# Middle weight bits by 16-bit copies on ScalarE, the first chunk's tap sums by float32 products on TensorE, and a rewritten opening list

## The chip, the cores and the metric

The kernel runs on one core of a Trainium2 chip. The metric is the device time of one execution in microseconds (us). The engines of the core are named as in the profile: PE is TensorE (products; PEld its weight loads), DVE is VectorE, ACT is ScalarE, POOL is GpSimd, and SP is SyncE, which issues most DMAs.

## The reference

The input x holds 8 sequences of 4160 rows of 192 numbers. Each row is replaced by a weighted sum over itself and the six rows before it, with seven weights ("taps") for each of 8 heads of 24 columns, after a softmax over the taps. Then three matrix products of 192 to 768 columns are taken, their elementwise maximum, and a product back to 192 columns. The matrices come in as 64-bit floats.

```
w = exp(weight_gen - max(weight_gen));  w = w / (sum(w) + 1e-9)     # over the 7 taps
out = einsum('bshk,bskhg->bshg', w, x_unf)                           # x_unf: rows s-6 .. s
h = maximum(maximum(out @ w1, out @ w2), out @ w3)
return h @ w_out
```

## The kernel before

**Tiling.** The 33,280 rows are 260 tiles of 128, one row on each partition; four tiles are a chunk of 512 rows, and there are 65 chunks. The rows of a partition are neighbours in the sequence, so that a tap is a shift along the tile xt. Inputs are loaded for a "super" at a time: the first is chunk 0 alone, the others are three chunks each.

**A chunk's path.** `softmax` works on a super (VectorE for the maxima, sums and reciprocals, GpSimd for the subtraction and the scaling, ScalarE for the exponentials). `product` (x in the list) multiplies a tile by its taps on GpSimd into r, 192 columns by 7 taps with the taps innermost, of which there are three buffers. `total` (+) sums the taps on VectorE into acc. `transpose` (t) turns acc so that the columns lie on the partitions: for chunks 0 to 2 on TensorE against a unit matrix, later on VectorE and ScalarE. `parts` (p) divides the result into float32 parts of fewer bits, xa_hi, xa_lo, xb and xc. `up` multiplies the parts by the weights' parts, nine steps of 18 products of 512 columns for a chunk: each product stands on 64 of 128 partitions, and the second half of the rows follows the first, so that two streams of products run beside each other. `maximum` takes the maxima (m) and their parts h_hi and h_lo; `down` multiplies by w_out and stores.

**The weights** come as 64-bit floats, viewed as two 32-bit words, low and high. `split` makes of each the part hi with 12 bits and the part lo with the next 24. It is called 18 times, all in the opening: nine times for wa (a in the list; 256 columns, from the tiles h_hi and raw_a, which hold raw words until later), three times for wb (b; 384 columns, from h_lo), six times for wo (d; 192 columns, from room). In each, ScalarE takes the absolute value (L467); three VectorE instructions make hi (L469, L471, L476), which ScalarE casts into place (L481); three more gather the 24 bits from both words (L483, L488) and the exponent (L492); ScalarE scales (L494) and GpSimd multiplies (L495). For wb four more casts on ScalarE put hi on both halves of the partitions (L550).

**Order.** Work is written in ticks, 22 to a chunk. What the steady table of ticks doesn't set, for chunks 0 to 4, stands in `OPENING`, a list by hand of the steps at each tick; -1 is before the first product. A name in it advances its step by one stage. `pin` keeps the order so written on each engine, and every engine works through its own queue in order. In `up`, the terms of one result are products in a fixed order.

Of the kernel before, what the change touches and what calls it, by code (L numbers as in the profile page):

```python
# [13 lines left out]
F32 = mybir.dt.float32  # L14
F32R = mybir.dt.float32r
U32 = mybir.dt.uint32
AF = mybir.ActivationFunctionType
ALU = mybir.AluOpType
AX = mybir.AxisListType

P = 128
# [3 lines left out]

OPENING = {
    -1: (
        "x0.0 s0 x0.1 a0 s0 a0 a0 x0.2 a0 a2 t0 +0.0 a2 b0 +0.1 a1 b0 b0 a1 +0.3 s1 a3 b0 a1 "
        "a2 s1 a1 +0.2 t0 b1 s1 x0.3"
    ),  # L30
    0: "a6 a4 a2 a3 a6",
    1: "a6 a3 b0 t0 t0",
    2: "b1 a6 s0",
    3: "a4 a5 a3",
    4: "b1 a5",
    6: "b2 +1.0 a5 x1.1 x1.0",
    7: "x1.2 s1 a4",
    8: "+1.1",
    9: "a5 b2 x1.3",
    10: "b2 b2 b1 p0",  # L40
    11: "s0 t1 +1.2",
    12: "a4 +1.3",
    14: "b1 p0",
    16: "a7 a7 a8 p1",
    17: "a7 t1",
    18: "s2 d1 d1 a8 p1",
    19: "p1 b2 a8 d2 t1",
    20: "d2 p0 d1",
    21: "d0",
    22: "d0",  # L50
    24: "a7 +2.0 d0",
    25: "d2 +2.1 d1",
    26: "d3 t1",
    27: "d0 x2.1 d3 d5 d2",
    28: "d3 x2.2",
    29: "x2.3 d3 a8 d4",
    30: "d4 x2.0",
    31: "d5",
    32: "+2.2 d4 d5",
    33: "t2 +2.3 t2 t2",  # L60
    34: "s2",
    35: "x3.0 x3.2 p2",
    36: "d4",
    38: "d5 p2 p2",
    42: "x3.1",
    43: "t3 t3",
    46: "+3.3 +3.2 +3.1 +3.0 t2",
    48: "t3",
    49: "s2",
    52: "x4.1",  # L70
    54: "t3",
    56: "x4.0 p3",
    57: "x3.3",
    58: "p3 t3 s2",
    59: "t3",
    61: "+4.1",
    66: "x4.2",
    67: "x4.3",
    68: "t3",
    69: "p3",  # L80
    74: "+4.3 +4.2",
    77: "+4.0",
}


# [7 lines left out]
LOAD = (5, 5)  # L93

ON_TENSOR = 3


@with_exitstack
def lightconv_maxout_kernel(
# [25 lines left out]
    nc = tc.nc  # L125
    B, S, D = x.shape
    H, K = weight_gen.shape[2:]
# [36 lines left out]
    ident = const.tile([P, P], F32, name="ident")  # L164
    wa_hi = const.tile([P, NJ, 3, P], F32R, name="wa_hi")
    wa_lo = const.tile([P, NJ, 3, P], F32R, name="wa_lo")
    wb_hi = const.tile([P, NJ, 3, P], F32R, name="wb_hi")
# [8 lines left out]
    state = {}  # L176

    def pin(ins):

        tc.keep_in_program_order(ins)  # L180
        return ins
# [28 lines left out]
    def softmax(s):  # L210
# [10 lines left out]
        yield  # L221
        pin(nc.scalar.activation(w3v, w3v, AF.Exp))
        yield
# [10 lines left out]
    def product(c, t):  # L234

        s = super_of[c]
        a, n = chunks[c]
        la = a - chunks[supers[s][0]][0]
        xt, wt = state["x", s], state["w", s]
        if t == 0:  # L240
            state["acc", c] = att.tile([P, TC, D], F32, name="acc")

        r = att.tile([P, D, K], F32, name="r", bufs=3)
        state["r", c, t] = r
        pin(
            nc.gpsimd.tensor_tensor(  # L246
                r.rearrange("p (h g) k -> p k h g", g=G),
                xt[:, la + t : la + t + K].rearrange("p k (h g) -> p k h g", g=G),
                wt[:, la + t]
                .rearrange("p (h k) -> p k h", k=K)  # L250
                .unsqueeze(3)
                .broadcast_to([P, K, H, G]),
                op=ALU.mult,
            )
        )

    def total(c, t):

        r = state.pop(("r", c, t))
        pin(  # L260
            nc.vector.tensor_reduce(  # L261
                state["acc", c][:, t], r, axis=AX.X, op=ALU.add
            )
        )

    def transpose(c):


        acc = state["acc", c]
        if c < ON_TENSOR:  # L270
            pa, pb = (ps.tile([P, CH], F32, name="ph") for _ in range(2))
            pb = pb[:DB]
            state["p", c] = pa, pb
            for t in range(TC):
                to = slice(t * P, (t + 1) * P)
                pin(nc.tensor.transpose(pa[:, to], acc[:, t, :P], ident))
                pin(nc.tensor.transpose(pb[:, to], acc[:, t, P:], ident))
                yield
            return
        v = xtp.tile([P, NJ * D * 2], F32, name="room", bufs=1)  # L280
        pa, pb = v[:, :CH], v[DB:, CH : 2 * CH]
        state["p", c] = pa, pb
        blocks = v[:, 2 * CH : 2 * CH + TC * D].rearrange("p (t d) -> p t d", t=TC)
        pin(nc.vector.transpose(blocks, acc))  # L284
        yield
        for f in range(0, D, 32):
            to = pa[f : f + 32] if f < P else pb[f - P : f - P + 32]
            to = to.rearrange("f (t p) -> f t p", t=TC)
            for p in range(0, P, 32):
                pin(nc.scalar.copy(to[:, :, p : p + 32], blocks[p : p + 32, :, f : f + 32]))  # L290
            yield

    def parts(c):
# [8 lines left out]

        eng, at = (nc.vector, halves[0]) if c < ON_TENSOR else (nc.gpsimd, halves[1])
        pin(eng.tensor_tensor(xa_lo, pa, xa_hi.bitcast(F32), op=ALU.subtract))  # L304
# [38 lines left out]
    def up(step, half):  # L343
        c, jp, i = step
        N = chunks[c][1] * P
        xa_hi, xa_lo, xb, xc = state["xT", c]
        for odd in range(2):
            j = 2 * jp + odd
            terms = [(wa_hi[:, j, i], xa_hi), (wa_hi[:, j, i], xa_lo), (wa_lo[:, j, i], xa_hi)]
            terms.append((wb_hi[:, j, i], xb))  # L350
            if half == odd:
                terms.append((wb_lo[:, jp, i], xc))
            if half == 0:
                state["ph", step, odd] = ps.tile([P, CH], F32, name="ph")
            terms = [(N, w, v[:, :N]) for w, v in terms]
            yield from product_of(state["ph", step, odd], terms, half, (step, odd))
            if half == 1:
                maximum(step, odd)
# [89 lines left out]

    words = [w.bitcast(U32) for w in (w1, w2, w3, w_out)]

    def split(raw, hi, lo):

        low, high = raw[..., 0], raw[..., 1]


        n = int(np.prod(raw.shape[1:-1]))
        if 2 * n <= CH:
            both = ps.tile([P, CH], F32, name="ph")
            u, l = both[:, :n], both[:, n : 2 * n]
        else:  # L460
            u, l = (ps.tile([P, CH], F32, name="ph")[:, :n] for _ in range(2))
        e, f = (prep.tile([P, NU], F32, name=name, bufs=3)[:, :n] for name in ("e", "f"))
        if len(raw.shape) == 4:
            u, l, e, f = (v.rearrange("p (i n) -> p i n", n=P) for v in (u, l, e, f))
        ui, li, ei = (v.bitcast(U32) for v in (u, l, e))

        pin(nc.scalar.activation(u, high.bitcast(F32), AF.Abs))  # L467
        yield
        pin(nc.vector.tensor_scalar(u, u, F_MAX, F_MIN, op0=ALU.min, op1=ALU.max))  # L469
        pin(  # L470
            nc.vector.tensor_scalar(  # L471
                ui, ui, 3, 0x3FFFF000, op0=ALU.logical_shift_left, op1=ALU.bitwise_and
            )
        )
        pin(
            nc.vector.scalar_tensor_tensor(  # L476
                ui, high, 0xC0000000, ui, op0=ALU.bitwise_and, op1=ALU.bitwise_or
            )
        )
        yield  # L480
        pin(nc.scalar.copy(hi, u))  # L481
        pin(
            nc.vector.tensor_scalar(  # L483
                li, high, 0x1FF, 15, op0=ALU.bitwise_and, op1=ALU.logical_shift_left
            )
        )
        pin(
            nc.vector.scalar_tensor_tensor(  # L488
                li, low, 17, li, op0=ALU.logical_shift_right, op1=ALU.bitwise_or
            )  # L490
        )
        pin(nc.vector.tensor_scalar(ei, ui, 0xFF800000, None, op0=ALU.bitwise_and))  # L492
        yield
        pin(nc.scalar.activation(f, li, AF.Copy, scale=2.0**-35))  # L494
        pin(nc.gpsimd.tensor_tensor(lo, f, e, op=ALU.mult))  # L495


    room = [
        hp.tile([P, NJ, CH], F32R, name=name).bitcast(U32).rearrange("p j n -> p (j n)")
        for name in ("h_hi", "h_lo")  # L500
# [4 lines left out]
        for r in (  # L505
            room[0][:, :SA],
            room[0][:, SA : 2 * SA],
            prep.tile([P, SA], U32, name="raw_a", bufs=1),
        )
    ]  # L510
    raw_b = room[1][:, : NJ * SB // 2].rearrange("p (j i n w) -> p j i n w", j=NJ // 2, i=3, w=2)
    raw_down = xtp.tile([P, NJ * D * 2], F32, name="room", bufs=1).bitcast(U32)
    raw_down = raw_down.rearrange("p (j n w) -> p j n w", j=NJ, w=2)
# [119 lines left out]
    for c in range(NC + 1):  # L633
        for tick in range(TICKS):
# [10 lines left out]
            k, odd = divmod(tick - (TC if tick >= 2 * DOWN_AT else 0), 2)  # L645
# [5 lines left out]
            if c == NC:  # L651
# [4 lines left out]
                elif tick >= 2 * DOWN_AT + TC and tick < 2 * DOWN_AT + 2 * TC:  # L656
                    t = tick - 2 * DOWN_AT - TC
# [44 lines left out]
```

## Time and profile before

| | us |
|---|---|
| median of 3 runs (1714.65 to 1714.75) | 1714.68 |
| profiled execution | 1714.73 |
| its span | 1712.9 |
| PE busy | 1668.9 (97%) |
| POOL busy | 1427.9 (83%) |
| ACT busy | 1138.6 (66%) |
| DVE busy | 1135.5 (66%) |

Busy time is the time in which an instruction of the engine ran; register, branch and DMA-issuing instructions don't count. Shares are over the whole span, so they mix the opening, in which weights are made ready, with the main stage. [...]

### The profile page before, as it was taken

What the parts mean: (1) busy time and instruction counts of PE and PEld (TensorE: products, weight loads), DVE (VectorE), ACT (ScalarE), POOL (GpSimd) and SP (SyncE); (2) the same over time, 40 slices, a digit from 0 to 9 for tenths busy, and PEclk for the clock granted to TensorE, in tenths of its full rate; (3) what the DMA queues carried; (4) which work ended last, traced back from release to release, by engine and by line L of the source; (5) the groups of instructions that cost most, each with busy time, mean ns of one, the idle gap of its engine ahead of it and who ended that gap; (6) DMA issues with size and microseconds to landing.
All of it is one profiled execution on the core that took longest, in us unless ns stands there. A gap on an engine that the chain in (4) does not pass through costs nothing.

```text
span 1712.9 us, 42123 instructions
## 1 busy us (share of the span) xinstructions
PE 1668.9 (97%) x16794; PEld 1639.7 (96%) x16794; DVE 1135.5 (66%) x1570; ACT 1138.6 (66%) x2878; POOL 1427.9 (83%) x844
## 2 busy tenths in 40 slices
PE   3799999999999999999999999999999999999999
PEld 2589999999999999999999999999999999999999
DVE  7967666666666666766666666666666666666653
ACT  3556667667667667666766766766766766676672
POOL 5888888989888888888888898988889888888872
PEclk9999999999999999999999999999999999999999
DMA  7010101101010110101010110101011010101000
GB/s 234 1 69 11 69 20 60 69 20 60 20 70 10 70 43 38 69 20 67 13 70 20 60 69 20 60 20 69 11 69 49 31 69 20 69 11 46 20 11 29
DMA packets 20422, 79.50 MB, mean 46 GB/s; under 512 B 2321, under 2 KB 5129, under 8 KB 17537
## 3 DMA queue, kind: packets, MB, share of 16 engines
q1 hardware_dynamic: 20104, 76.54, 11.8%
q8 instruction: 131, 2.15, 0.5%
q14 instruction: 67, 0.54, 0.1%
q10 hardware_dynamic: 120, 0.28, 0.1%
HBM read 51.25 MB, written 25.56 MB: 45 GB/s over the span
## 4 chain that ended last, share of the span: by engine, by line
PE 94%; DVE 4%; DMA 1%; issue 0%; SPq 0%; ACT 0%; DVEq 0%; ACTq 0%
PE ph L329 94%; DVE acc L261 1%; DVE m L378 1%; DVE ph L471 0%; DVE e L492 0%; DVE ph L476 0%; DMA h_lo<-in_moe_w_dram 0%; DVE ph L488 0%; DVE ph L469 0%; DVE ph L483 0%; DMA xt<-in_x_dram 0%; SPq L526 0%; DVE red L215 0%; SPq L518 0%; DVE xb L309 0%
## 5 line engine op out<-in xcount | busy, mean ns | idle before, releaser
L246 POOL TENSOR_TENSOR r<-xt,wt 128x1344 f32<-128x1344 f32 x260 | 721.8, 2817 | 0.7 <-DMA xt<-in_x_dram 0.4
L378 DVE TENSOR_TENSOR m<-ph,m 128x512 f32<-128x512 f32 x780 | 522.8, 685 | 215.4 <-PE ph L329 115.8
L385 POOL TENSOR_TENSOR h_lo<-m,h_hi 128x512 fp32r<-128x512 f32 x390 | 503.3, 1302 | 169.3 <-ACT h_hi L381 164.5
L329 PE MATMUL ph<-xa_hi,wa_hi 64*128 64x512 f32 x2340 | 627.5, 390 | 5.6 <-ACT f L494 3.4
L329 PE MATMUL ph<-xa_lo,wa_hi 64*128 64x512 f32 x2340 | 624.8, 388 | 2.5 <-DVE xa_lo L304 2.5
L329 PE MATMUL ph<-xa_hi,wa_lo 64*128 64x512 f32 x2340 | 624.3, 388 | 2.8 <-POOL wa_lo L495 2.7
L329 PE MATMUL ph<-xb,wb_hi 64*128 64x512 f32 x2340 | 623.9, 387 | 0.0
L329 PE MATMUL ph<-wo,h_hi 64*128 64x384 f32 x3120 | 596.1, 358 | 0.0
L329 PE MATMUL ph<-wo,h_lo 64*128 64x192 f32 x3120 | 554.9, 249 | 0.0
L381 ACT CAST h_hi<-m 128x512 fp32r<-128x512 f32 x390 | 242.0, 621 | 403.9 <-DVE m L378 400.9
L329 PEld LDWEIGHTS ph<-wo,h_hi 64*128 64x128 f32 x3120 | 486.3, 184 | 7.3 <-POOL wo L495 0.2
L329 PEld LDWEIGHTS ph<-wo,h_lo 64*128 64x128 f32 x3120 | 484.8, 187 | 0.1
L261 DVE TENSOR_REDUCE acc<-r 128x192 f32<-128x1344 f32 x260 | 401.9, 1547 | 109.7 <-POOL r L246 109.7
L290 ACT COPY room<-room 32x128 f32<-32x128 f32 x1488 | 440.6, 296 | 26.7 <-DVE room L284 8.5
L329 PE MATMUL ph<-xc,wb_lo 64*128 64x512 f32 x1170 | 453.3, 387 | 1.4 <-POOL wb_lo L495 1.4
L329 PEld LDWEIGHTS ph<-xa_hi,wa_hi 64*128 64x128 f32 x2340 | 364.3, 185 | 12.7 <-ACT f L494 4.2
L329 PEld LDWEIGHTS ph<-xa_hi,wa_lo 64*128 64x128 f32 x2340 | 357.6, 185 | 6.8 <-POOL wa_lo L495 4.4
L329 PEld LDWEIGHTS ph<-xa_lo,wa_hi 64*128 64x128 f32 x2340 | 357.6, 185 | 5.1 <-DVE xa_lo L304 3.0
L329 PEld LDWEIGHTS ph<-xb,wb_hi 64*128 64x128 f32 x2340 | 357.8, 185 | 2.5
L376 ACT COPY m<-ph 128x512 f32<-128x512 f32 x390 | 222.0, 586 | 57.1 <-PE ph L329 49.6
L411 DVE TENSOR_TENSOR o<-ph,ob 128x192 f32<-128x192 f32 x260 | 86.5, 353 | 237.5 <-ACT ob L410 237.5
L329 PEld LDWEIGHTS ph<-xc,wb_lo 64*128 64x128 f32 x1170 | 216.0, 185 | 3.6 <-POOL wb_lo L495 1.8
(57 smaller groups left out, 699.7 us busy)
## 6 DMA issues: line engine op xcount, KB each, us to landing
xt<-in_x_dram SPq DMA_DIRECT2D x20, 1728.0 KB, 6.8
out_dram<-o SPq DMA_DIRECT2D x64, 384.0 KB, 2.3
wt<-in_weight_gen_dram SPq DMA_DIRECT2D x21, 336.0 KB, 3.0
h_hi<-in_moe_w_dram SPq DMA_DIRECT2D x6, 256.0 KB, 5.5
xt<-in_x_dram SPq DMA_DIRECT2D x1, 1536.0 KB, 9.3
h_lo<-in_moe_w_dram SPq DMA_DIRECT2D x6, 192.0 KB, 5.6
room<-in_moe_w_out_dram SPq DMA_DIRECT2D x1, 1152.0 KB, 7.6
xt<-in_x_dram SPq DMA_DIRECT2D x1, 960.0 KB, 5.1
```

Source lines behind the costliest of these rows:

```text
L246: nc.gpsimd.tensor_tensor(r.rearrange("p (h g) k -> p k h g", g=G), xt[:, la + t : la + t + K].rearrange("p k (h g) -> p k h g", g=G), wt[ ...
L261: nc.vector.tensor_reduce(state["acc", c][:, t], r, axis=AX.X, op=ALU.add)
L290: pin(nc.scalar.copy(to[:, :, p : p + 32], blocks[p : p + 32, :, f : f + 32]))
L329: ins = nc.tensor.matmul(ph[:, :n], w[h], v[h], start=begins and half == 0 and q == 0, stop=ends and half == 1 and q == len(terms) - 1,)
L376: pin(nc.scalar.copy(m[:, :N], ph[:, :N]))
L378: pin(nc.vector.tensor_tensor(m[:, :N], ph[:, :N], m[:, :N], op=ALU.max))
L381: later(1, lambda: pin(nc.scalar.copy(hi, m[:, :N])))
L385: nc.gpsimd.tensor_tensor(lo, m[:, :N], hi.bitcast(F32), op=ALU.subtract)
L411: pin(nc.vector.tensor_tensor(o[:, t], po[:, :D], ob, op=ALU.add))
```

## The change

There are four edits. `split` no longer shifts and joins the two words on VectorE. ScalarE copies the two middle 16-bit quarters of each 64-bit number, as numbers of 16 bits, into the tile f, and one VectorE instruction masks them there; the factor of the scaling is halved, since the bits now stand one place higher. For chunk 0 `total` does nothing: `transpose` takes the taps' products r themselves as the weights of seven float32 products with the unit matrix, which add up in PSUM, twice for each tile (128 and 64 columns). In `up` the product with wa_lo goes to the end of its terms. And `OPENING` is written anew from tick -1 to 82.

```diff
 OPENING = {
     -1: (
-        "x0.0 s0 x0.1 a0 s0 a0 a0 x0.2 a0 a2 t0 +0.0 a2 b0 +0.1 a1 b0 b0 a1 +0.3 s1 a3 b0 a1 "
-        "a2 s1 a1 +0.2 t0 b1 s1 x0.3"
+        "x0.0 x0.1 a0 a0 a2 x0.3 t0 a0 a1 a0 a2 t0 a2 x0.2 t0 b0 b0 a2 b0 s1 a1 a1 b0 t0 s1 "
+        "b1 a1 s1 a3 s0"
     ),
...
+SUMS_ON_TENSOR = (0,)
...
-        if t == 0:
+        if t == 0 and c not in SUMS_ON_TENSOR:
             state["acc", c] = att.tile([P, TC, D], F32, name="acc")
...
     def total(c, t):
 
+        if c in SUMS_ON_TENSOR:
+            return
...
-                pin(nc.tensor.transpose(pa[:, to], acc[:, t, :P], ident))
-                pin(nc.tensor.transpose(pb[:, to], acc[:, t, P:], ident))
+                if c in SUMS_ON_TENSOR:
+                    r = state.pop(("r", c, t))
+                    for k in range(K):
+                        for ph, f in ((pa, slice(0, P)), (pb, slice(P, D))):
+                            pin(
+                                nc.tensor.matmul(
+                                    ph[:, to], r[:, f, k], ident, start=k == 0, stop=k == K - 1
+                                )
+                            )
+                else:
+                    pin(nc.tensor.transpose(pa[:, to], acc[:, t, :P], ident))
+                    pin(nc.tensor.transpose(pb[:, to], acc[:, t, P:], ident))
...
-            terms = [(wa_hi[:, j, i], xa_hi), (wa_hi[:, j, i], xa_lo), (wa_lo[:, j, i], xa_hi)]
-            terms.append((wb_hi[:, j, i], xb))
+            terms = [(wa_hi[:, j, i], xa_hi), (wa_hi[:, j, i], xa_lo), (wb_hi[:, j, i], xb)]
             if half == odd:
                 terms.append((wb_lo[:, jp, i], xc))
+            terms.append((wa_lo[:, j, i], xa_hi))
...
         pin(nc.scalar.activation(u, high.bitcast(F32), AF.Abs))
         yield
+        flat = raw.rearrange("p i n w -> p (i n) w") if len(raw.shape) == 4 else raw
+        pin(
+            nc.scalar.copy(
+                f_words.bitcast(U16).rearrange("p (n h) -> p n h", h=2),
+                flat.bitcast(U16)[..., 1:3],
+            )
+        )
...
-        pin(
-            nc.vector.tensor_scalar(
-                li, high, 0x1FF, 15, op0=ALU.bitwise_and, op1=ALU.logical_shift_left
-            )
-        )
-        pin(
-            nc.vector.scalar_tensor_tensor(
-                li, low, 17, li, op0=ALU.logical_shift_right, op1=ALU.bitwise_or
-            )
-        )
+        pin(nc.vector.tensor_scalar(li, f.bitcast(U32), 0x01FFFFFE, None, op0=ALU.bitwise_and))
...
-        pin(nc.scalar.activation(f, li, AF.Copy, scale=2.0**-35))
+        pin(nc.scalar.activation(f, li, AF.Copy, scale=2.0**-36))
```

On VectorE, from the end of the first wa split to the first wb split (the wb words are in h_lo), there stood before:

```order
L492 TENSOR_SCALAR e<-ph 128x256
L261 TENSOR_REDUCE acc<-r 128x192
L469 TENSOR_SCALAR ph<-ph 128x256
L471 TENSOR_SCALAR ph<-ph 128x256
L476 SCALAR_TENSOR_TENSOR ph<-h_hi,ph 128x256
L261 TENSOR_REDUCE acc<-r 128x192
L469 TENSOR_SCALAR ph<-ph 128x384
L471 TENSOR_SCALAR ph<-ph 128x384
L476 SCALAR_TENSOR_TENSOR ph<-h_lo,ph 128x384
L483 TENSOR_SCALAR ph<-h_lo 128x384
L488 SCALAR_TENSOR_TENSOR ph<-h_lo,ph 128x384
L492 TENSOR_SCALAR e<-ph 128x384
```

Now there stands on VectorE, at the same place:

```order
L506 TENSOR_SCALAR e<-ph 128x256
L492 TENSOR_SCALAR ph<-ph 128x256
L494 TENSOR_SCALAR ph<-ph 128x256
L499 SCALAR_TENSOR_TENSOR ph<-h_hi,ph 128x256
L505 TENSOR_SCALAR ph<-f 128x256
L506 TENSOR_SCALAR e<-ph 128x256
L492 TENSOR_SCALAR ph<-ph 128x384
L494 TENSOR_SCALAR ph<-ph 128x384
L499 SCALAR_TENSOR_TENSOR ph<-h_lo,ph 128x384
L505 TENSOR_SCALAR ph<-f 128x384
L506 TENSOR_SCALAR e<-ph 128x384
L216 TENSOR_REDUCE red<-wt 128x96
```

The two sums of chunk 0 are gone, the second wa split is finished ahead of the wb split, both splits have five instructions and not six, and the maximum of the second softmax (red) follows at once.

On ScalarE, around the first wb split, from its absolute value on, there stood before, with the exponentials of the second softmax as the last row:

```order
L467 ACTIVATE ph<-h_lo 128x384
L467 ACTIVATE ph<-h_hi 128x256
L481 CAST hi<-ph 128x384
L467 ACTIVATE ph<-h_hi 128x256
L494 ACTIVATE f<-ph 128x384
L550 CAST wb_hi<-hi 64x384 x4
L481 CAST wa_hi<-ph 128x2x128 x2
L222 ACTIVATE wt<-wt 128x672
```

Now, on ScalarE at that place:

```order
L481 ACTIVATE ph<-h_lo 128x384
L487 COPY f<-h_lo 128x768
L508 ACTIVATE f<-ph 128x256
L504 CAST hi<-ph 128x384
L487 COPY f<-h_hi 128x512
L504 CAST wa_hi<-ph 128x2x128
L508 ACTIVATE f<-ph 128x384
L564 CAST wb_hi<-hi 64x384 x4
L223 ACTIVATE wt<-wt 128x672
```

Copies of 16-bit numbers have come in, and the cast of a wa split (wa_hi) stands ahead of the wb casts, no longer behind them.

On TensorE, where the transposes of chunk 0 end and its first products begin, there stood before (xa, xb and xc are the parts of chunk 0):

```order
L276 MATMUL ph<-ident,acc 128x128
L277 MATMUL ph<-ident,acc 64x128
L329 MATMUL ph<-xa_hi,wa_hi 128x512
L329 MATMUL ph<-xa_lo,wa_hi 128x512
L329 MATMUL ph<-xa_hi,wa_lo 128x512
L329 MATMUL ph<-xb,wb_hi 128x512
L329 MATMUL ph<-xc,wb_lo 128x512
```

Now, on TensorE there, the last two of 56 float32 products and then the first terms:

```order
L284 MATMUL ph<-ident,r 128x128
L284 MATMUL ph<-ident,r 64x128
L342 MATMUL ph<-xa_hi,wa_hi 128x512
L342 MATMUL ph<-xa_lo,wa_hi 128x512
L342 MATMUL ph<-xb,wb_hi 128x512
L342 MATMUL ph<-xc,wb_lo 128x512
L342 MATMUL ph<-xa_hi,wa_lo 128x512
```

The transposes of chunk 0 have become products that read r, and wa_lo is now read last.

## Rows read from the trace of the kernel before

**Rows 1.** Stretches: start:end and length, busy us (instructions) by engine, granted clock, DMA.

```profile
30.00:40.00 10.00, 7.46 (x28) 5.48 (x29) 9.38 (x22) 4.11 (x10) 3.71 (x4) 1.00 0.67 259
40.00:50.00 10.00, 6.17 (x44) 4.10 (x43) 9.79 (x18) 5.35 (x12) 9.12 (x6) 1.00 0.00 0
...
60.00:70.00 10.00, 6.68 (x40) 4.46 (x42) 9.52 (x23) 6.00 (x14) 7.45 (x6) 0.83 0.00 0
...
200.00:1600.00 1400.00, 1400.00 (x14242) 1394.03 (x14240) 926.53 (x1237) 961.59 (x2446) 1208.20 (x700) 1.00 0.11 44
```

**Rows 2.** Chain of work that ended last: start us, us, what.

```profile
10.65 6.09 DMA h_lo<-in_moe_w_dram
...
17.44 0.58 DVE ph L469
...
175.85 1533.65 PE ph L329 x12937
```

**Rows 3.** Waits of DVE from 9 to 92 us: us in total, times, longest.

```profile
DVE ph L469 <- ACT ph L467: 3.3, 2, 2.3
```

**Rows 4.** DVE in order of time: start us, us, engine, line, operation.

```profile
20.64 0.42 DVE L469 TENSOR_SCALAR ph<-ph 128x256 f32<-128x256 f32 x1
...
42.08 0.68 DVE L378 TENSOR_TENSOR m<-ph,m 128x512 f32<-128x512 f32 x1
...
58.92 0.43 DVE L488 SCALAR_TENSOR_TENSOR ph<-raw_a,ph 128x256 uint32<-128x256 uint32 x1
59.38 0.42 DVE L492 TENSOR_SCALAR e<-ph 128x256 uint32<-128x256 uint32 x1
...
87.53 1.54 DVE L261 TENSOR_REDUCE acc<-r 128x192 f32<-128x1344 f32 x1
89.00 2.47 DVE L378 TENSOR_TENSOR m<-ph,m 128x512 f32<-128x512 f32 x4
```

**Rows 5.** ACT and DVE in order of time, around the second softmax.

```profile
20.30 0.49 ACT L494 ACTIVATE f<-ph 128x384 f32<-128x384 uint32 x1 [0.28 <-DVE ph L488]
20.68 2.06 ACT L550 CAST wb_hi<-hi 64x384 fp32r<-64x384 f32 x4
...
25.68 0.76 ACT L222 ACTIVATE wt<-wt 128x672 f32<-128x672 f32 x1 [2.26 <-POOL wt L217]
...
28.09 0.84 DVE L224 TENSOR_REDUCE den<-wt 128x96 f32<-128x672 f32 x1
...
29.89 0.41 DVE L469 TENSOR_SCALAR ph<-ph 128x256 f32<-128x256 f32 x1
```

**Rows 6.** Groups by line and shape, 8 to 90 us: count, busy us, mean ns, idle before.

```profile
L381 ACT CAST h_hi<-m 128x512 fp32r<-128x512 f32 x8 | 5.0, 620 | 8.4 <-DVE m L378 8.3
...
L494 ACT ACTIVATE f<-ph 128x256 f32<-128x256 uint32 x9 | 3.3, 378 | 4.7 <-DVE e L492 4.7
...
L488 DVE SCALAR_TENSOR_TENSOR ph<-room,ph 128x192 uint32<-128x192 uint32 x6 | 2.2, 362 | 0.2
```

**Rows 7.** PE in order of time: the last transposes of chunk 0, and products.

```profile
28.71 0.42 PE L276 MATMUL ph<-ident,acc 128*128 128x128 f32 x1
28.93 0.42 PE L277 MATMUL ph<-ident,acc 128*64 128x128 f32 x1
...
34.15 0.62 PE L329 MATMUL ph<-xb,wb_hi 64*128 64x512 f32 x1
34.58 0.62 PE L329 MATMUL ph<-xc,wb_lo 64*128 64x512 f32 x1
...
40.99 0.39 PE L329 MATMUL ph<-xa_hi,wa_hi 64*128 64x512 f32 x1
...
41.22 0.39 PE L329 MATMUL ph<-xa_lo,wa_hi 64*128 64x512 f32 x1
```

**Rows 8.** POOL in order of time: the first three products of the taps.

```profile
7.86 7.65 POOL L246 TENSOR_TENSOR r<-xt,wt 128x1344 f32<-128x1344 f32 x3 [0.37 <-DMA xt<-in_x_dram]
```

**Rows 9.** PE in order of time: the last wait ahead of its unbroken run.

```profile
85.56 0.33 PE L276 MATMUL ph<-ident,acc 128*128 128x128 f32 x1 [0.87 <-DVE acc L261]
```

More of the change, by code (lines that the diff above doesn't have):

```diff
@@ L16 @@
 U32 = mybir.dt.uint32
+U16 = mybir.dt.uint16
 AF = mybir.ActivationFunctionType
@@ L27 @@
     -1: (
-        "x0.0 s0 x0.1 a0 s0 a0 a0 x0.2 a0 a2 t0 +0.0 a2 b0 +0.1 a1 b0 b0 a1 +0.3 s1 a3 b0 a1 "
-        "a2 s1 a1 +0.2 t0 b1 s1 x0.3"
-    ),
[L31 to L65, printed above, removed]
-    43: "t3 t3",
[L67 to L82, printed above, removed]
+        "x0.0 x0.1 a0 a0 a2 x0.3 t0 a0 a1 a0 a2 t0 a2 x0.2 t0 b0 b0 a2 b0 s1 a1 a1 b0 t0 s1 "
+        "b1 a1 s1 a3 s0"
+    ),
+    0: "a3 a6 b1 a3 a6",
+    1: "a6 +1.0 a4 x1.2 a6",
+    2: "s0",
+    3: "a3 b1 a5",
+    4: "a4 a5",
+    5: "x1.0 a4",
+    6: "b2 x1.1 a5 b0",
+    7: "b1",
+    8: "+1.1 s1 a4 x1.3 a5",
+    9: "s0 b2",
+    10: "b2 +1.3",
+    11: "a7 +1.2 t1 s0",
+    14: "p0 b2 p0",
+    16: "a7 a8 p1",
+    17: "t1 a7 a8 p0",
+    18: "a7 d1 s2 p1",
+    19: "b1 a8 p1 d2",
+    20: "d2",
+    21: "d1 d1 d0",
+    22: "b2 d0",
+    24: "+2.0 d1",
+    25: "d0 d2 +2.1",
+    27: "d0 t1 d3",
+    28: "a8 d2 x2.2 x2.3 d3 d5",
+    29: "d3 d4",
+    30: "d3",
+    31: "x2.1 d5 d4",
+    32: "+2.2 s2",
+    33: "t2 t2 d5 d4",
+    34: "x2.0 +2.3 t2 t1",
+    35: "x3.0 p2 x3.1",
+    37: "p2 p2",
+    38: "d4 d5",
+    43: "t3 t3",
+    46: "+3.3",
+    47: "+3.0 +3.2",
+    48: "t3 +3.1",
+    49: "x4.1 s2",
+    52: "t3",
+    54: "t3 t2",
+    55: "p3",
+    58: "x4.0 s2",
+    63: "+4.1",
+    65: "p3",
+    66: "t3 x4.2",
+    67: "x4.3 t3",
+    68: "+4.2",
+    76: "x3.3 +4.0",
+    79: "+4.3 x3.2",
+    82: "p3",
 }
@@ L266, in transpose @@
     def transpose(c):
-        acc = state["acc", c]
+        acc = state.get(("acc", c))
         if c < ON_TENSOR:
@@ L451, in split @@
     def split(raw, hi, lo):
-        low, high = raw[..., 0], raw[..., 1]
+        high = raw[..., 1]
         n = int(np.prod(raw.shape[1:-1]))
@@ L462, in split @@
         e, f = (prep.tile([P, NU], F32, name=name, bufs=3)[:, :n] for name in ("e", "f"))
+        f_words = f
         if len(raw.shape) == 4:
```

## The prediction

> **What bounds the kernel now.** I read the stretches first, then the chain of work that ended last, then the waits of each engine, and last the instructions one by one in the stretches that matter. From 200 to 1600 us TensorE is busy for all of 1400.00 us [rows 1], and the chain of work that ended last is one unbroken piece of TensorE from 175.85 us for 1533.65 us [rows 2]. Nothing that relieves another engine can be worth anything there; the products of the main stage stay as many and as long as they are. What can be gained lies in the first 90 us. There VectorE is busy 9.4 to 9.8 us of every 10, while TensorE has 7.5, 6.2 and 6.7 [rows 1]. The chain says the same: VectorE's pieces follow one another from 17.44 us on [rows 2]. Between 9 and 92 us VectorE waited for ScalarE's first step of a split 3.3 us in all, twice [rows 3]; the second of these is 1.0 us just ahead of 17.44, when the wb words, which landed at 16.7 (10.65 + 6.09) [rows 2], had first to pass ScalarE. After 17.44 it waits for nobody until its last opening work, the fourth sum of chunk 2, ends at 89.00 [rows 4]. The last idle time of TensorE ahead of its unbroken run is at 85.56: 0.87 us, ended by VectorE's third sum of chunk 2 [rows 9]. So the opening lasts as long as VectorE's list, and the kernel gets shorter by as much as that list, in time and not in work, gets shorter between 17.44 and 85.5 to 89.
>
> **What VectorE loses.** Two things. The four sums of chunk 0: one sum takes 87.53 to 89.00, 1.47 us [rows 4]; four are 5.9 us. And one of six VectorE instructions of each of the 18 splits (9 of wa, 3 of wb, 6 of wo): the second word instruction begins 0.46 us before the next at 256 columns, 58.92 to 59.38 [rows 4]; at 192 columns it lasts 0.36 [rows 6], with the same 0.03 or 0.04 around it 0.40. With 0.46 also for the three wider ones that is 12 x 0.46 + 6 x 0.40 = 7.9 us. In all 13.8 us of work. The one that stays reads a copy in SBUF and masks it in place of masking and shifting the source; I price it as the one that it replaces.
>
> **What of it can't be used.** Two of the four sums lie ahead of 17.44, and there the list now runs into the load of the wb words, which is issued in the same place and lands as before. The new list puts the second half of the next wa split (two instructions) there, and idles for the rest. So what counts is the work from 17.44 to 89.00, 71.6 us without a gap. From it go two sums (2.9), the three instructions of that split's second half, now ahead of 17.44 (1.3), and 16 second-word instructions (10 x 0.46 + 6 x 0.40 = 7.0); the new list has one more maximum ahead of the last sum (0.6, a quarter of the four that took 2.47 [rows 4]). 71.6 - 2.9 - 1.3 - 7.0 + 0.6 = 61.0 us: 10.6 us less, if VectorE never waits.
>
> **Where it will wait.** First, for ScalarE at the denominators of the second softmax. The first wb split took from 17.44 to the next group at 20.64 [rows 4]; less one instruction it ends at 20.2. With the maximum over the taps (0.8, as long as the sum of the same shape at 28.09 [rows 5]) and the five instructions of a wa split (2.1) VectorE is there at 23.1. The exponentials must come first, and in ScalarE's new order they stand behind that wa split's cast, which can't begin before VectorE's third instruction at 22.3, then a scaling (0.4 from 20.30 to 20.68) and the four wb casts (2.1): 22.3 + 0.3 (the cast, 0.38 long as its like [rows 6], overlapping a little) + 0.4 + 2.1 + 0.8 for the exponentials [rows 5] = 25.9. VectorE waits 2.8 us. Second, for TensorE at the first maximum, which ran at 42.08 [rows 4]. From 25.9 VectorE has three softmax instructions (1.8, 28.09 to 29.89 [rows 5]) and eleven of splits (5.0), so it comes to the two parts of chunk 0 at 32.7 and leaves them at 34.1, about as before; the first products, at the same pace, bring that maximum to about 42.3. VectorE is there after one sum and twelve instructions of splits (6.6), at 40.7, and waits 1.6 us. The sum: 10.6 - 2.8 - 1.6 = 6.2 us. Three things ride along at nothing. The order of the terms moves the wa_lo product to the end of its group in all 65 chunks: the same shapes in the same number, so no change where TensorE never waits, and a little slack in the opening, where GpSimd makes wa_lo last. The DMA queue's list is the same. GpSimd, 9.1 of 10 us busy from 40 to 50 [rows 1], comes to its products for chunk 1 earlier, since two wa_lo fewer stand ahead of the second softmax's scaling in its queue, and has no more to do.
>
> **What ScalarE gets.** 18 copies of 512, 768 or 384 16-bit numbers. No row shows one. Nearest is the cast of 512 float32 numbers between SBUF tiles, 0.62 us; the lower bound is the 0.38 of 256 [rows 6], if two 16-bit numbers count as one, the upper twice the former. I take 0.62 for 512, and in proportion 0.9 and 0.5: 9 x 0.62 + 3 x 0.9 + 6 x 0.5 = 11.3 us, on an engine that is busy 5.4 and 6.0 us of 10 [rows 1]. They stand ahead of the casts that wait for VectorE anyway; the three ahead of the parts of chunk 0 still let them go at 30.0. Twice the price moves that to 32 or 33 and costs 1 to 3 us.
>
> **What TensorE gets.** 56 float32 products of 128 columns for 8 transposes. They must be done by 30.0, when ScalarE is free for the parts; until then VectorE has other work, and that is the cover. The first product tile is there at 10.4 (7.86 + a third of 7.65) [rows 8]. No row has a float32 product that isn't a transpose. Transposes of this shape follow each other at 0.22 us (28.71 to 28.93): the lower bound. A product of 512 columns follows the next at 0.43 early (34.15 to 34.58) and at 0.23 later (40.99 to 41.22, one of two streams). If nothing overlaps, a transpose's 0.42 and its weight load of half that make 0.65, the upper bound [rows 7]. [...] I take 0.43, falling to 0.21 after 7 us: the plain product has to multiply all bits of both operands, so it is nearer to the longer row. The first 14 end at 16.4, 3 more bring 17.8, 39 at 0.21 end at 26. The fourth product tile waits for the first's buffer, 16.4 and not 15.5: 1 us of GpSimd, hidden. With the clock never rising it is 10.4 + 56 x 0.43 = 34.5: VectorE's second part, which needs two casts more (1.9), begins at 36.3 and not 33.4, 2.9 us lost. At 0.22 throughout nothing changes.
>
> [...]
>
> **The rivals.** [...] (2) Slower: the same cover fails further. The clock stays low, the weight load, whose columns lie 28 bytes apart in the product tile, isn't hidden, and a product takes the upper bound: 10.4 + 56 x 0.65 = 46.8, VectorE's second part at 48.7, 15.3 us late, 1714.7 - 6.2 + 15.3 = 1724. VectorE and TensorE both stand still for it. It decides against the change from a mean of (10.4 + 27.4) on: 27.4 / 56 = 0.49 us per product, where the parts are 6.2 us late. Speaking for it: the transposes near 28 us ran at 0.22 [rows 7], no faster than a low clock explains. (3) The two waits above don't come, the parts being prepared for a TensorE that is already at its high clock: 10.6 us, 1704. Against it: after its idle times TensorE got less clock (0.83 from 60 to 70, where it was busy 6.68 us of 10 [rows 1]), and the float32 products are followed by an idle time again. (4) The list's time is saved but not passed on: with less slack, in-order queues of ScalarE and GpSimd hold up casts and wa_lo, and half is lost: 3 us, 1711.7.
>
> **How the numbers follow.** The profiled execution took 1714.73 us with a span of 1712.9; the median of the runs is 1714.68, so the sum can be set against either. 1714.7 - 6.2 = 1708.5; its own range, with the prices of copies and the clock, is 1706 to 1711. Chances: forecast 0.47, (3) 0.12, (4) 0.13, (1) 0.13, (2) 0.15. The range takes in all but (2) and the best of (3): 1703 to 1718. 0.2% is 3.4 us, about what a measurement of this kernel can tell from no change. Faster than 1711.3: forecast, (3) and a third of (4), 0.64. Within: the rest of (4) and most of (1), 0.20. Slower: (2) and a little of (1), 0.16.
>
> **What would show it.** Right: VectorE's fourth sum of chunk 2 ends near 83 and not 89; the float32 products end before 30; VectorE waits for the exponentials from 23 to 26; TensorE's unbroken run starts near 79 and not 85.6; the main stage's pace as before, 1400.00 / 14242 x 258 = 25.4 us for the 258 products of a chunk [rows 1]. Wrong, if the last float32 product ends after 30 and VectorE's parts wait for it; if copies of 512 take over 1 us; or if the main stage's pace changes with the order of the terms, where 0.1% would already be 1.6 us.

## The result, and the profile after

The changed kernel took 1727.57 us (median of 4 runs, 1727.23 to 1728.34) beside 1714.66 us of the kernel before (1714.53 to 1714.75): a ratio of 1.0076 (time over time of before), 95% interval 1.0060 to 1.0092. It is 12.9 us slower; the prediction said 6.2 us faster. The profiled execution took 1727.77 us, with a span of 1726.0.

The stretches of the kernel after, with the columns of [rows 1], show that the main stage is as it was and that the loss lies in the opening:

```profile
20.00:30.00 10.00, 10.00 (x30) 6.03 (x30) 4.54 (x9) 5.99 (x14) 6.94 (x6) 1.00 0.74 237
30.00:40.00 10.00, 10.00 (x31) 6.04 (x29) 5.08 (x12) 1.45 (x3) 4.00 (x2) 1.00 0.62 256
40.00:50.00 10.00, 9.95 (x29) 6.05 (x29) 0.33 (x1) 0.91 (x2) 2.62 (x1) 1.00 0.00 0
...
200.00:1600.00 1400.00, 1400.00 (x14242) 1392.21 (x14240) 925.87 (x1232) 964.01 (x2454) 1209.63 (x700) 1.00 0.12 44
```

From 200 to 1600 us TensorE does 14242 instructions in 1400.00 us, as before [rows 1]. From 40 to 50 us the engines have changed places: VectorE, busy 9.79 of 10 before [rows 1], is busy 0.33; TensorE, 6.17 before, is busy 9.95, with 29 instructions only.

The chain of work that ended last says what these are (start, length, what):

```profile
10.74 38.91 PE ph L284 x112
49.67 0.58 ACT xc L319
...
51.55 4.72 PE ph L342 x12
...
99.50 2.11 PE ph L342 x16
```

L284 is the line of the float32 products. In the chain of before VectorE's split stood from 17.44 on [rows 2]; now the products fill 38.9 us without a gap. TensorE's last wait of the opening ends at 99.50 and not at 85.56 [rows 9]: 13.9 us later, where the time is 12.9 us longer.

The groups of the two unit-matrix tiles tell the price (instructions, shortest/median/longest ns, first and last start, shapes):

```profile
L284 PEld LDWEIGHTS ph<-ident,r x112: 190/258/328, 10.7 to 49.0; 128*128 128x128 f32 x56, 128*64 128x64 f32 x56
L284 PE MATMUL ph<-ident,r x112: 417/460/598, 10.7 to 49.2; 128*128 128x128 f32 x56, 128*64 128x128 f32 x56
```

The program has 56 of these products, the trace 112, each with a weight load: a float32 product stands there as two passes. 38.91 / 56 = 0.695 us a product, 0.347 a pass. The pace never changes: 30, 31 and 29 instructions in the three stretches of 10 us above.

Who waits is in the waits of VectorE from 9 to 110 us (total, times, longest):

```profile
DVE xa_lo L317 <- ACT xa_hi L313: 14.3, 1, 14.3
DVE ph L505 <- ACT wa_hi L504: 6.0, 5, 3.0
DVE ph L492 <- ACT ph L481: 4.1, 2, 2.8
DVE den L225 <- ACT wt L223: 2.2, 1, 2.2
```

and in the order of time on ScalarE and VectorE:

```profile
49.05 0.59 ACT L313 CAST xa_hi<-ph 128x512 fp32r<-128x512 f32 x1 [16.53 <-PE ph L284]
...
49.67 0.69 DVE L317 TENSOR_TENSOR xa_lo<-ph,xa_hi 128x512 fp32r<-128x512 f32 x1 [14.28 <-ACT xa_hi L313]
...
50.89 0.69 DVE L322 TENSOR_TENSOR xb<-ph,xc 64x512 fp32r<-64x512 f32 x1 [0.53 <-ACT xc L319]
...
99.44 1.54 DVE L264 TENSOR_REDUCE acc<-r 128x192 f32<-128x1344 f32 x1
```

ScalarE is ready for the parts of chunk 0 at 32.5 and stands 16.53 us for the products; VectorE stands 14.28 us behind ScalarE. The fourth sum of chunk 2, VectorE's last opening work, starts at 99.44 and not at 87.53 [rows 4]. Both engines work through their queues in order, and nothing from behind the parts ran in that time: in the row from 40 to 50 us above VectorE has one instruction and ScalarE two, all of them of the parts.

### The profile page after: what moved, and what is told of

Its sections match the earlier page's. It is cut to its first block, busy times and chain, and to the rows that moved or that the text cites. A ratio compares the mean times of both kernels' runs of the same rounds, so it can differ in the third digit from the quotient of the medians.

```text
span 1726.0 us, 42392 instructions
## 1 busy us (share of the span) xinstructions
PE 1701.8 (99%) x16898; PEld 1659.4 (96%) x16898; DVE 1123.9 (65%) x1548; ACT 1147.0 (66%) x2896; POOL 1428.7 (83%) x844
## 4 chain that ended last, share of the span: by engine, by line
PE 96%; DVE 2%; ACT 0%; DMA 0%; POOL 0%; issue 0%; SPq 0%; DVEq 0%; POOLq 0%; ACTq 0%
PE ph L342 94%; PE ph L284 2%; DVE acc L264 1%; DVE m L391 1%; DMA xt<-in_x_dram 0%; POOL r L247 0%; DVE e L506 0%; DVE ph L494 0%; DVE ph L499 0%; DVE ph L505 0%; DVE ph L492 0%; ACT xc L319 0%; ACT m L389 0%; ACT xb L321 0%; ACT f L487 0%
## 5 line engine op out<-in xcount | busy, mean ns | idle before, releaser
L264 DVE TENSOR_REDUCE acc<-r 128x192 f32<-128x1344 f32 x256 | 395.6, 1547 | 109.6 <-POOL r L247 109.5
```

The lines of the kernel that those rows point to most:

```text
L264: nc.vector.tensor_reduce(state["acc", c][:, t], r, axis=AX.X, op=ALU.add)
```

## The experiments

The theory after the result, **A**: the loss is the end of the float32 products, past what other work covers. The rivals: the copies or the new list cost the time; the order of the terms slows the main stage; the weight loads' stride makes the products slow; the clock alone makes them slow. The time of before in the three sets of runs was 1714.54, 1714.58 and 1714.37 us. Behind each measured time stand in brackets the ratio to before and its 95% interval. In what was expected of the runs on the clock, the letters C and D mean other theories from one run to the next.

**The parts of the change by themselves.** First, the change without the sums on TensorE (VectorE sums chunk 0 again, early in the new list):

```diff
-        "x0.0 x0.1 a0 a0 a2 x0.3 t0 a0 a1 a0 a2 t0 a2 x0.2 t0 b0 b0 a2 b0 s1 a1 a1 b0 t0 s1 "
+        "x0.0 x0.1 a0 a0 a2 x0.3 +0.0 t0 a0 a1 a0 a2 +0.1 t0 a2 x0.2 +0.2 t0 b0 b0 a2 b0 s1 a1 a1 b0 "
+        "+0.3 t0 s1 "
...
-SUMS_ON_TENSOR = (0,)
+SUMS_ON_TENSOR = ()
```

> The changed kernel with the four sums of chunk 0 back on VectorE, each ahead of its transposes in the new list; copies, order of the terms and the rest of the list as changed. Theory A, the float32 products are the whole loss: VectorE comes to the parts of chunk 0 near 33 to 36 us, since two to three of its four sums fall into waits that it has there anyway, its fourth sum of chunk 2 ends near 84 to 87 and not 101, and the time is 1709 to 1713 us. Theory B, the copies or the new list lose by themselves: the parts are not much later than 36 either, but the opening still ends past 89 and the time is over 1716 us.

Second, the kernel before with the copies alone:

```diff
...
+            nc.scalar.copy(
+                f_words.bitcast(U16).rearrange("p (n h) -> p n h", h=2),
+                flat.bitcast(U16)[..., 1:3],
+            )
...
+        pin(nc.vector.tensor_scalar(li, f.bitcast(U32), 0x01FFFFFE, None, op0=ALU.bitwise_and))
...
```

> The kernel before with the 16-bit copies alone; old list, old order of the terms, sums on VectorE. Theory A, VectorE's list sets the opening and 17 of its 18 instructions saved lie in the gapless stretch: 7.4 us at most, 1707.3, less 1 to 3 us for waits on ScalarE: 1707 to 1711 us, fourth sum of chunk 2 near 82 to 85. Theory B, ScalarE's 11 us of copies stand in front of what VectorE waits for: 1713 us or more, with waits of VectorE for ScalarE that add up to as much as it saves.

Third, the kernel before with the sums on TensorE alone:

```diff
+SUMS_ON_TENSOR = (0,)
...
```

> The kernel before with the sums of chunk 0 as float32 products alone; old list, old splits. Theory A: 56 products at 0.695 us end at 49.7, VectorE stands at the parts of chunk 0 from about 30 on and goes on at 50 in place of 32.4, which is 17 to 18 us late; what it saved ahead of that is lost in the same wait, so 1731 to 1733 us. Theory B, the loss comes from the new list or the copies: under 1722 us.

Fourth, the kernel before with the wa_lo product last in its terms, alone:

```diff
...
+            terms.append((wa_lo[:, j, i], xa_hi))
```

> The kernel before with the wa_lo product moved to the end of its terms, nothing else. Theory A: the same products in the same number, TensorE waits 2.7 us for wa_lo in the whole opening and VectorE's list sets its end: 1713 to 1715 us. Theory B, the order changes the pace of the main stage by 0.1% or more: 1.6 us or more either way, seen in the busy time of all chunks from 200 us on.

Measured: without the sums 1713.04 (ratio 0.9992, interval 0.9984 to 1.0001); copies alone 1710.67 (0.9979, 0.9970 to 0.9987); sums alone 1733.19 (1.0109, 1.0094 to 1.0125); order of the terms alone 1714.46 (0.9999, 0.9990 to 1.0008). All four came as theory A expected, the first and the third at the upper end of its range or up to 0.2 us above. The loss goes with the sums: without them the change is no slower than before. Copies alone are worth 3.9 us. In the run with the sums alone the wait for the products is longer than in the change, since VectorE's queue is the old one (its waits):

```profile
DVE xa_lo L318 <- ACT xa_hi L314: 19.7, 1, 19.7
```

and with the copies alone VectorE comes sooner to the fourth sum of chunk 2:

```profile
83.14 1.54 DVE L262 TENSOR_REDUCE acc<-r 128x192 f32<-128x1344 f32 x1
```

4.4 us before 87.53 [rows 4], for 3.9 us of time. The order of the terms left 1400.00 us and 14243 instructions in the main stage.

**The stride of the weight loads.** In r the taps are innermost, so the 128 columns of a weight load lie 28 bytes apart. Here r of chunk 0 has the taps outermost:

```diff
+        if c in SUMS_ON_TENSOR:
+            r = r.rearrange("p d k -> p (d k)").rearrange("p (k d) -> p d k", k=K)
```

> The changed kernel, but for chunk 0 the taps lie outermost in the product tile, so that the 128 or 64 columns of a weight load are neighbours and not 28 bytes apart. Theory S, the stride of the load is a good part of the 0.695 us of a float32 product: the 56 products fall from 38.9 to 25 to 31 us and the time by as much, 1716 to 1720 us. Theory F, the form costs it, two passes at the low clock whatever the layout: 38 to 39 us, 1727 to 1728 us.

Measured: 1726.97 us (1.0072, 1.0056 to 1.0087), and the products in order of time:

```profile
10.65 37.78 PE L286 MATMUL ph<-ident,r 128*128 128x128 f32 x112 [10.65 <-POOL r L249]
```

37.8 us in place of 38.9: the stride costs 0.02 us a product, theory F's size and not theory S's. It isn't the cause.

**Fewer bits.** r of chunk 0 and the unit matrix as fp32r:

```diff
+    ident_r = const.tile([P, P], F32R, name="ident_r")
...
-        r = att.tile([P, D, K], F32, name="r", bufs=3)
+        r = att.tile([P, D, K], F32R if c in SUMS_ON_TENSOR else F32, name="r", bufs=3)
...
```

> The changed kernel with the products of chunk 0's taps and the unit matrix held as fp32r, a float32 of fewer bits, so the sums of chunk 0 lose accuracy; everything else as changed. Theory F, a plain float32 product is two passes and this one: 56 passes in place of 112, at 0.35 us 19.5 us, ending at 31, 1708 to 1712 us. If the columns or the clock set the time and not the passes, 30 us or more and over 1718 us.

Measured: 1710.43 us (0.9977, 0.9967 to 0.9987). In order of time, the sums, VectorE's fourth sum of chunk 2, and TensorE's last wait of the opening:

```profile
10.47 10.45 PE L284 MATMUL ph<-ident_r,r 128*128 128x128 f32 x56 [10.47 <-POOL r L247]
...
81.74 1.54 DVE L264 TENSOR_REDUCE acc<-r 128x192 f32<-128x1344 f32 x1
...
81.80 0.41 PE L342 MATMUL ph<-wo,h_hi 64*128 64x384 f32 x1 [0.86 <-ACT f L508]
```

One record each, 10.45 / 56 = 0.187 us. The time came as expected, but not the price: two passes of float32 against one of fp32r would have made 0.35 us, and an fp32r product takes about a quarter of 0.695, not half. So the number of records doesn't give the price. With the price gone, the rest of the change does about what was forecast of it: the last sum ends at 83.3, where the prediction said near 83.

**How the time follows the number of products.** Five and three of the seven taps for chunk 0, everything else as in the change:

```diff
-                    for k in range(K):
+                    for k in range(5):
...
```

> After, but for chunk 0 only five of the seven taps are multiplied on TensorE (two taps' share is missing from that chunk's result): 40 float32 products in place of 56. Theory A, the time follows the end of the float32 products, microsecond for microsecond: 40 x 0.695 = 27.8 us, end at 38.5 in place of 49.67, VectorE's fourth sum of chunk 2 from 99.4 to some 88.3, time 1727.6 - 11.1 = 1716.5 (by the prediction's own working, 1708.5 + 38.5 - 31.5 = 1715.5): about the point at which the change stops paying. Theory B, what comes behind the sums (GpSimd's and VectorE's bunched work) costs the time by itself: above 1722.

> After, but for chunk 0 only three of the seven taps are multiplied on TensorE (four taps' share is missing from that chunk's result): 24 float32 products. Theory A: 24 x 0.695 = 16.7 us, end at 27.4, ahead of 30.0, where ScalarE is free for the parts; so the products are covered, and the time is that of the run with fp32r sums, 1710.4 (1709.5 to 1711.5), fourth sum of chunk 2 at about 81.7. Theory B, no cover, every microsecond earlier still counts: 1727.6 - 22.3 = 1705.3.

Measured: 1716.29 us with five taps (1.0012, 1.0003 to 1.0021), 1709.75 with three (0.9973, 0.9963 to 0.9984). The products with five taps:

```profile
10.76 27.80 PE L284 MATMUL ph<-ident,r 128*128 128x128 f32 x80 [10.76 <-POOL r L247]
```

and with three, with the parts of chunk 0 behind them and the fourth sum of chunk 2:

```profile
10.51 16.71 PE L284 MATMUL ph<-ident,r 128*128 128x128 f32 x48 [10.51 <-POOL r L247]
...
29.75 0.59 ACT L313 CAST xa_hi<-ph 128x512 fp32r<-128x512 f32 x1
...
33.34 0.68 DVE L322 TENSOR_TENSOR xb<-ph,xc 64x512 fp32r<-64x512 f32 x1
...
81.97 1.54 DVE L264 TENSOR_REDUCE acc<-r 128x192 f32<-128x1344 f32 x1
```

From 56 products to 40 the end falls by 11.1 us (49.65 to 38.56) and the time by 11.3: one for one, theory A. From 40 to 24 it falls by 11.3 more and the time by 6.5 only: here the cover begins. The cast xa_hi of the run with three taps has no wait ahead of it any more. At one for one from five taps on, 1709.75 would be met where the products end at 38.56 - 6.54 = 32.0; that is the cover by these times. The time of before, 1714.4, would be met at an end of 36.6, or (36.6 - 10.7) / 56 = 0.46 us a product; the prediction's deciding point was 0.49.

**The clock.** 28 products of 512 bf16 columns, on zeros, ahead of the sums:

```diff
...
+    early = const.tile([P, CH], mybir.dt.bfloat16, name="early")
+    nc.gpsimd.memset(early, 0.0)
+    spare = ps.tile([P, CH], F32, name="ph")
+    for _ in range(28):
+        pin(nc.tensor.matmul(spare, early[:, :P], early, start=True, stop=True))
```

> The changed kernel with 28 products of 512 columns on a bfloat16 tile of zeros put ahead of the sums on TensorE, where it idles till 10.7 us; their result isn't used. Theory C, the low clock is half the price and the sums keep a clock that was raised for them: 0.17 us per pass, 56 products in about 20 us, parts of chunk 0 no later than 33 us, 1708 to 1712 us. Theory D, float32 products of this shape don't keep it up: the pace falls back to 0.35 per pass within some us, the products take 33 to 38 us and the time is 1721 to 1728 us.

> The same kernel as the one with 28 bf16 products on zeros ahead of the sums, once more. If a run of the faster sort (1718.5 to 1719.7) is the profiled one, theory A wants the float32 products to end some 8 us sooner than 48.9, at about 41, with the higher pace, 0.22 us a record, lasting well past 13.6; if it is of the other sort (1727), the products end near 48.9 and the higher pace ends near 13.6 again.

Measured: 1719.70 us (1.0046, 1.0028 to 1.0064), and once more 1719.22 (1.0036, 1.0023 to 1.0048). The times fall into two groups, 1717.8 to 1719.7 us and 1726.1 to 1727.6; of 15 in all, 11 are in the first. The mean granted clock on record is 0.996 to 0.999 in those 11 and 0.987 or 0.988 in the other four. The first profile is of one of the second group, of 1726.82 us. Its stretches, with the instructions of the sums alone (busy us and count of PE, PEld, POOL, then granted clock and DMA):

```profile
11.00:13.00 2.00, 2.00 (x9) 1.52 (x9) 0.00 (x0) 1.00 1.07 222
13.00:15.00 2.00, 2.00 (x7) 1.36 (x7) 0.00 (x0) 0.68 1.14 243
15.00:17.00 2.00, 2.00 (x7) 1.14 (x7) 0.00 (x0) 0.50 1.06 245
...
20.00:30.00 10.00, 10.00 (x30) 6.14 (x29) 0.00 (x0) 0.50 0.68 225
```

The granted clock, a share of full speed, is 1.00 when the float32 products begin, and some 3 us later it falls to 0.50, though TensorE had no gap (busy all of each stretch); it stays there, and reads 0.50 from 40 to 50 us too. The second profile is of one of the first group, of 1719.22 us. The same view, and the products in order of time:

```profile
10.00:20.00 10.00, 9.52 (x35) 7.47 (x36) 0.00 (x0) 1.00 1.09 302
20.00:30.00 10.00, 10.00 (x38) 7.74 (x38) 0.00 (x0) 1.00 0.68 225
30.00:40.00 10.00, 10.00 (x38) 7.79 (x37) 0.00 (x0) 1.00 0.74 291
```

```profile
10.48 30.50 PE L284 MATMUL ph<-ident,r 128*128 128x128 f32 x112 [1.23 <-POOL r L247]
```

Here the upper level held to the end: 30.50 / 56 = 0.545 us a product, 0.272 a pass and not theory C's 0.17. Theory D's fall came in the first profile and not in the second. In the change itself the granted clock reads 1.00 through the sums, but 30 instructions in 10 us are the pace of the 0.50 stretch above and not of the 1.00 stretch, 38; I go by the pace. The first product of 512 columns behind the sums bears it out, as far as the profile's ends of products, which are modelled, can. In the first profile, at 0.50, then in the second, at 1.00, then in the change:

```profile
48.94 0.79 PE L342 MATMUL ph<-xa_hi,wa_hi 64*128 64x512 f32 x1
...
41.23 0.50 PE L342 MATMUL ph<-xa_hi,wa_hi 64*128 64x512 f32 x1 [0.24 <-ACT xa_hi L313]
...
49.69 0.79 PE L342 MATMUL ph<-xa_hi,wa_hi 64*128 64x512 f32 x1
```

So by these paces the low clock costs, as an estimate, (0.695 - 0.545) x 56 = 8.4 us of the change. The other part isn't the clock's: at the upper level the products end at 40.98, 9.0 us behind the cover, and 1709.75 + 9.0 = 1718.7 stands beside 1719.2 measured.

**Type or shape?** The fp32r sums, with each product made four times against a quarter of the unit matrix:

```diff
-                    for k in range(K):
+                    for k in range(4 * K):
...
-                                    ph[:, to], r[:, f, k], ident_r, start=k == 0, stop=k == K - 1
+                                    ph[:, to], r[:, f, k // 4], ident_r, start=k == 0, stop=k == 4 * K - 1
...
```

> The run with fp32r sums for chunk 0 (fewer bits), but each product is made four times, with a quarter of the unit matrix: 224 passes of 128 columns, each with its own weight load, in place of 56. Theory C, TensorE's clock stays low under short products whatever their type: 224 x 0.187 = 41.9 us, end at 52.4, time about 1727.6 + 2.7 = 1730. Theory D, it stays low because of the float32 form alone: the pace rises after some 7 us from 0.187 to about 0.1 us, 37 passes to 17.4 and 187 x 0.1 = 18.7 more, end at 36, late against 31.5 by 4.6, time about 1715.

Measured: 1728.68 us (1.0083, 1.0068 to 1.0098). In order of time:

```profile
10.42 39.46 PE L284 MATMUL ph<-ident_r,r 128*128 128x128 f32 x224 [10.42 <-POOL r L247]
```

and in stretches, with these instructions alone (PE, PEld, DVE, granted clock, DMA):

```profile
20.00:25.00 5.00, 5.00 (x31) 5.00 (x29) 0.00 (x0) 1.00 0.56 203
...
35.00:40.00 5.00, 5.00 (x31) 5.00 (x30) 0.00 (x0) 1.00 0.29 122
```

0.176 us a pass, the same from the first stretch to the last. Theory D's rise to 0.1 us didn't come; theory C's 1730 is within 1.3 us. So a pace that stays flat isn't peculiar to float32. The granted clock reads 1.00 here too, but the first product of 512 columns behind these passes takes what it takes at 0.50:

```profile
50.43 0.79 PE L342 MATMUL ph<-xa_hi,wa_hi 64*128 64x512 f32 x1 [0.56 <-ACT xa_hi L313]
```

By this row the clock was low when the passes ended. What such a pass would take at the upper level no run shows; the weight loads (PEld) are busy for all of 5.00 us already. Four passes make 0.705 us, one float32 product 0.695.

**A version that keeps the gain.** The kernel before with the copies, and one tile of chunk 0 only (the third to be multiplied) summed by float32 products:

```diff
+SUMS_ON_TENSOR = ((0, 2),)
...
+        if (c, t) in SUMS_ON_TENSOR:
+            return
...
```

> The kernel before with the copies, and of chunk 0 only the third tile's sum as 14 float32 products; the other three sums on VectorE, old list. By theory A 14 products take 9.7 us and end near 27, ahead of the fourth tile's sum, so they are covered, and VectorE has 1.5 us less in its gapless stretch than with the copies alone: 1708.5 to 1710 us, fourth sum of chunk 2 near 81.7. If VectorE's list isn't what counts: 1710.7 as with the copies alone, or slower where the products end after 28.

Measured: 1710.12 us (0.9975, 0.9966 to 0.9984). In order of time:

```profile
16.18 9.60 PE L286 MATMUL ph<-ident,r 128*128 128x128 f32 x28
...
81.25 1.54 DVE L266 TENSOR_REDUCE acc<-r 128x192 f32<-128x1344 f32 x1
```

14 products end at 25.8, ahead of the cover. The time is 4.5 us below before and 17.5 below the change. Against the copies alone it is 0.5 us better, which lies within the intervals of the two, so that the one tile's sum adds nothing that is clear of noise.

## Why the prediction was wrong, point by point

- **What bounds the kernel: right.** Wherever the products left room, the time followed VectorE's opening list. The start of the fourth sum of chunk 2 against 87.53 [rows 4], and the time against before: copies alone -4.4 and -3.9, one tile -6.3 and -4.5, fp32r sums -5.8 and -4.2, three taps -5.6 and -4.6, the change +11.9 and +12.9, sums alone (start at 105.99) +18.5 and +18.7.
- **The price of a float32 product: wrong, and the step that failed.** The prediction took 0.43 us, "falling to 0.21 after 7 us", for an end at 26. Measured is 0.695, flat, for an end at 49.65. Two things were mis-sized. The larger is the product itself: I chose the spacing of a 512-column fp32r product as the nearest row, but a float32 product costs about what four fp32r passes of its size cost (0.695 beside 4 x 0.176), and even at the upper clock, 0.545, the products ended at 40.98 and not at 26. The other is the rise of the clock after 7 us, carried over from products of 512 columns (0.43 us apart at 34.15, 0.23 at 40.99 [rows 7], a rise read from the pace, since the granted clock from 30 to 40 us is 1.00 [rows 1]) to a shape on which no row showed one; the pace didn't rise in 38.9 us, which made about 41 into 49.65. No run shows a float32 product at 0.21 us or a price that falls after 7 us; the runs showed 0.695 from first to last in the change and 0.545 in the second profile behind bf16 products. That the plain product multiplies all bits of both operands was my reason for the longer row; no run shows it.
- **The upper bound was too low.** 0.65 us, a transpose's time [rows 7] and half of it for the load (0.17 to 0.23 us at 28 us in the trace of before), was meant as an end; the measured 0.695 lies above it. Here a bound built on a transpose didn't hold for a product, which took 3.2 times the 0.22 at which the transposes near 28 us followed each other. In time a product is near four fp32r passes (0.695 beside 4 x 0.176), though the traces show two records for it.
- **The rivals.** Rival 2 came, in its course: a clock that stays low (by the pace), products that outlast the cover, and VectorE's parts late by as much. It gave 46.8 for the end of the products, 48.7 for VectorE's second part, and 1724. Measured are 49.65, 50.89 and 1727.6. With the measured start of the second part, 17.5 us behind 33.4, its formula gives 1714.7 - 6.2 + 17.5 = 1726.0. But its reason for the price, the stride of the load, was wrong: 37.8 us without it. That its price came near was luck. Its chance, 0.15, was too small for what spoke for it (transposes 0.22 us apart near 28 us, where those of before at 55.94 and 56.05 are 0.11 apart), and the range left it out.
- **The cover: right.** ScalarE was to be free for the parts at 30.0, and with three taps its cast begins at 29.75. The working of late products started from 31.5 (33.4 - 1.9); the times give 32.0.
- **The buffer of the fourth product tile: mis-sized.** It was put at 1 us of GpSimd, hidden, with a start at 16.4. In the change it starts at 20.67:

```profile
20.67 2.62 POOL L247 TENSOR_TENSOR r<-xt,wt 128x1344 f32<-128x1344 f32 x1 [4.91 <-PE ph L284]
```

  The exponentials came at 27.21, where three taps had 24.54, and ScalarE was ready at 32.5 and not at 29.75. No cost of it shows in the time, since the products kept ScalarE waiting 16.53 us more.
- **What VectorE loses and where it waits: nearly right in sum.** With the products covered, the forecast was 6.2 us and an end of 1708.5; three taps gave 4.6, fp32r sums 4.2 by 1710.4. VectorE's list was shorter by 5.6 to 5.8. In the run with three taps the wait at the denominators was 2.2 for 2.8. The first maximum came at 42.13 for 42.3, but VectorE didn't wait there for TensorE: it came late itself, after 1.45 us of waiting for ScalarE's cast in a split, in place of the 1.6:

```profile
25.34 0.85 DVE L225 TENSOR_REDUCE den<-wt 128x96 f32<-128x672 f32 x1 [2.17 <-ACT wt L223]
...
41.25 0.43 DVE L505 TENSOR_SCALAR ph<-f 128x256 uint32<-128x256 uint32 x1 [1.45 <-ACT wa_hi L504]
...
42.13 0.68 DVE L391 TENSOR_TENSOR m<-ph,m 128x512 f32<-128x512 f32 x1
```

  So that sum came out in part by luck. TensorE's last wait ended at 81.80 with fp32r sums and not near 79, for a scaling on ScalarE.

- **The copies: right.** By their groups in the kernel after, from 5 to 90 us (count, busy us, mean ns):

```profile
L487 ACT COPY f<-h_hi 128x512 uint16<-128x512 uint16 x6 | 3.6, 613 | 4.7 <-POOL wa_lo L509 4.7
L487 ACT COPY f<-h_lo 128x768 uint16<-128x768 uint16 x3 | 2.5, 820 | 0.0
L487 ACT COPY f<-room 128x384 uint16<-128x384 uint16 x4 | 2.1, 517 | 0.0
```

  0.61, 0.82 and 0.52 us, where 0.62, 0.9 and 0.5 were taken.
- **The order of the terms: right**, nothing by itself.
- **The new list** wasn't costed alone. With the copies but without the sums on TensorE it gives 1713.0, where the old list with the copies gives 1710.7. I placed the sums in it by hand, so whether the list itself costs these 2.4 us isn't shown.

Left open: why the granted clock, once at 1.00, held through the sums in one profiled run behind bf16 products and fell to 0.50 in the other (by their times and mean clocks 11 of the 15 runs are like the one and four like the other); why a float32 product with two records takes as long as four fp32r passes (0.695 beside 0.705); and which step ate the 1 to 2 us between VectorE's gain and the time's.

## What to carry to other kernels

Before a sum goes to TensorE as float32 products, price them at what a product of that very shape and type costs, not at a transpose's or a wider product's pace: here 0.695 us for 128 columns, where a transpose of before took 0.22 and a product of 512 columns 0.43 or 0.23 [rows 7], against 1.47 for VectorE's sum of a whole tile, which took 14 of them. Where no row shows such a product, let the range take in the slowest reading. Find the time by which the result must be there, and the price at which that is missed; beyond it every microsecond was paid in full (11.1 for 11.3). Where a change has parts, the part that saves work on the bound engine and adds it to one with idle time can be the whole gain: the copies alone gave 3.9 us of the 4.5 that the version with one tile had, and the rest isn't clear of noise.

## What the runs showed of the hardware that was not expected

A float32 product that isn't a transpose stands in the trace as two products with two weight loads, 0.347 us a pass at the lower clock and 0.272 at the upper: the higher clock saved about a fifth. It costs about what four fp32r passes of its size cost (0.695 beside 4 x 0.176). The pace of the change's sums never rose in 38.9 us without a gap, and the product behind them took 0.79 us, as at a granted clock of 0.50. Behind bf16 products, whose pace had risen (9 of them between 1 and 5 us, 16 between 5 and 9), the granted clock fell from 1.00 to 0.50 some 3 us into the sums in one profiled run and not in the other of the same program. A granted clock that reads 1.00 was no proof of the upper level: at 1.00 the change's sums ran at the pace of a stretch at 0.50 (30 instructions in 10 us), where the second profile behind bf16 products had 38. And weight loads of float32 columns 28 bytes apart cost nearly the same as of neighbours, 38.9 beside 37.8 us for 56 products.
